# Column softmax of the first three batches from a ScalarE copy of the scores, in place of a second set of products

## The chip, the cores and the metric

The kernel runs on one core of a Trainium2 chip. The metric is the device time of one execution in microseconds (us). Times inside an execution come from the hardware profiler: they count from the start of the profiled span. The engines are named as the profile names them: PE (TensorE, matrix products; PEld its weight loads), DVE (VectorE), ACT (ScalarE), POOL (GpSimd) and SP (SyncE, which here only issues the stores).

## What is computed

Eight batches of an attention read in two directions, followed by a two-layer network with a squared ReLU:

```python
# x [8, 8, 512, 64], state [8, 8, 32, 64]: batch, head, token or state row, 64
scores  = scale * x @ state.T            # [.., 512, 32]
xread   = softmax(scores, rows)  @ state   # row softmax, over 32 state rows
scores2 = scale * state @ x.T            # [.., 32, 512]: the same scores, turned
sread   = softmax(scores2, rows) @ x       # column softmax, over 512 tokens
t = concat([xread, sread])               # 544 tokens a batch, heads side by side: [4352, 512]
out = (s * relu(t @ w_in)**2 + b) @ w_out  # 512 -> 2048 -> 512
```

The scores of both reads are the same numbers. The kernel makes them once per use, in a tile T of 128 partitions (4 heads x 32 state rows) by 2 groups x 512 tokens, fp32, in two banks of PSUM. T serves the row softmax (through a transpose) and, as it stands, the column softmax.

## The kernel before

The order of all instructions on every engine is written out by hand. The first stretch (lines 583 to 671) is a straight list for batches 0 and 1. Then the loop of lines 752 to 805 emits eight phases, b = 0 to 7. Phase b has sixteen steps (`phase`, line 674). A step runs the pieces that the lists `before` and `behind` hold for its number, then one slice of layer 1 for batch b + 1 (`layer1_x`: 2 matmuls into hps, a ReLU by ACT from hps to r), and every second step a square by DVE (`square`, r to g). Layer 2 of batch b (`layer2`, 4 matmuls of g with w_out into ops) is spread over the steps as pieces. In phases 6 and 7 layer 2 is computed with seven half-size products in place of eight (`fast_layer2`, products X, Y and W into opf tiles, sums of g by DVE). Phase 7 runs layer 1 of the sread rows. hps has two PSUM buffers, so the layer-1 slice i needs the ReLU of slice i - 2 done; r has five buffers.

The row softmax of batch b + 2 is a chain (`chain`, line 690), placed within phase b: `at_T` (16 small PE matmuls, T from stE and xT), `at_U` (DVE transposes T out of PSUM), `at_mu` (row maxima), `at_D` (Dm = U - mu), `at_E1` (ACT exponential), `at_z` (row sums and reciprocals), `at_At` and `at_A` (the weights A, scaled and transposed back by DVE). A is the moving operand of layer 1; its stationary operand M = state @ w_in (per head) is made by `at_M` (16 matmuls into mps) and copied to SBUF by `at_Mc`. xT is x transposed in 32 x 32 blocks by DVE (`at_xT`).

The column softmax of a batch is `at_nm` (DVE: maximum over 512 tokens, negated and scaled, nm and nms), `at_E2` (two ACT exponentials E of 512 columns that also give the sums rs), `at_a2` (DVE: times the reciprocal), `at_a2T` (8 PE transposes into aps and a copy), `at_V` (32 matmuls with x rows xn into vps) and `at_srd` (ACT copy into srdT). For batches 3 to 7 these pieces follow in the same phase as the chain, while T still stands in PSUM. For batches 0, 1 and 2 they run later, through `late` (line 707): batch 2 in phase 3 and batches 0 and 1 in phase 6. There T is long overwritten, so `late` begins with a second `at_T(b)` from a kept xT. The tiles xT_0, xT_1 and xT_2 have buffers of their own for that (lines 231 to 234); xT_3 and later share one.

T lives in either of two pairs of PSUM banks, made by `two_banks`: one (tag pt) for T and some M tiles, one (tag pa) for the second half of batch 0's T, most M tiles, aps and vps. PE's matmuls of a new tile there wait until the tile before it has been read.

In the first stretch batch 0 is done in two halves of its tokens (`at_T(0, 0)` in pt, `at_T(0, 1)` in pa). PE runs filler matmuls between (`idle`, tile dps). The weights w_in come in four DMAs from POOL's queue, and `at_M2(0, 2)` and `at_M2(0, 3)` need the last two.

Of the kernel before, what the change touches and what calls it, by code (L numbers as in the profile page):

```python
# [10 lines left out]
FP32 = mybir.dt.float32  # L11
FP16 = mybir.dt.float16
# [3 lines left out]
def kernel(  # L16
# [12 lines left out]
    nc = tc.nc  # L29
    AF = mybir.ActivationFunctionType  # L30
    ALU = mybir.AluOpType
    AX = mybir.AxisListType

    B, H, S, D = x.shape
# [3 lines left out]
    P = 128  # L38
    NK = DM // P
    NKF = DF // P  # L40
    NG = H // 4
# [10 lines left out]
    konst = ctx.enter_context(tc.tile_pool(name="konst", bufs=1))  # L52
    wpool = ctx.enter_context(tc.tile_pool(name="wpool", bufs=1))
    xpool = ctx.enter_context(tc.tile_pool(name="xpool", bufs=2))
    apool = ctx.enter_context(tc.tile_pool(name="apool", bufs=1))
# [30 lines left out]
    act, dve = nc.scalar.copy, nc.vector.tensor_copy  # L86
# [81 lines left out]
    def w_out_f(f):  # L168
        return w_out16[:, f, :]
# [34 lines left out]
    at = [dict() for _ in range(B)]  # L204
# [8 lines left out]
    def part(t, p=None, g=None):  # L213

        if g is not None:
            t = t[:, g : g + 1]
        if p is not None:
            n = t.shape[2] // 2
            t = t[:, :, n * p : n * p + n]
        return t  # L220
# [7 lines left out]
    def at_xT(b, g=None, p=None):  # L228

        if "xT" not in at[b]:  # L230
            keep = b < 3
            at[b]["xT"] = (konst if keep else apool).tile(
                [P, NG, S, 2], FP16, name=f"xT_{b}", tag=f"xTk{b}" if keep else "xT"
            )
        out = at[b]["xT"].rearrange("p g s e -> p g (s e)").bitcast(FP32)
        in_ = xh_t[b].rearrange("p g j d -> p g (j d)").bitcast(FP32)
        nc.vector.transpose(part(out, p, g), part(in_, p, g))  # L237

    def at_T(b, p=None):

        half = p is not None
        at[b]["T"] = T = two_banks(f"T_{b}", own=not p)
        for e in range(2):
            for hp in range(4):
                for g in range(NG):
                    r = hp ^ g
                    mm(
                        part(T[Ns * hp : Ns * hp + Ns], p, g)[:, 0, :],
                        stE[32 * r : 32 * r + 32, NG * b + g, :, e],
                        part(at[b]["xT"][32 * r : 32 * r + 32, :, :, e], p, g)[:, 0, :],  # L250
                        start=(e == 0), stop=(e == 1),
                        tp=(32 * r, Ns * hp),
                    )

    def at_U(b, p=None, g=None):
        U = sm(b, "U", [P, NG, S], FP32)
# [48 lines left out]

    def at_nm(b):
        nm, nms = sm(b, "nm", [P, NG], FP32), sm(b, "nms", [P, NG], FP32)
        nc.vector.tensor_reduce(  # L308
            nm, at[b]["T"], AX.X, ALU.max, negate=True
        )  # L310
        nc.vector.tensor_scalar(nms, nm, scale, None, ALU.mult)  # L311

    def at_E2(b, gs=range(NG)):
        E2, rs = sm(b, "E2", [P, NG, S], FP16), sm(b, "rs", [P, NG], FP32)
        for g in gs:
            nc.scalar.activation(  # L316
                E2[:, g], at[b]["T"][:, g], AF.Exp,
                bias=at[b]["nms"][:, g : g + 1], scale=scale, accum_out=rs[:, g : g + 1],
            )

# [88 lines left out]
    def layer1_half(b, f, p):  # L409

        M, A = at[b]["M"], at[b]["A"]
        hps = ps_h.tile([P, 2, HALF], FP32, name=f"hph_{b}_{f}_{p}", tag="ph")
        for i in range(2):
            for g in range(NG):
                lhsT = M[:, g, P * (f + i) : P * (f + i) + P]
                mm(hps[:, i, :], lhsT, part(A, p, g)[:, 0, :], start=(g == 0), stop=(g == NG - 1))
        r = R_t[b, f, p] = rpool.tile([P, 2, HALF], FP16, name=f"rh_{b}_{f}_{p}", tag="r")
        nc.scalar.activation(r, hps, AF.Relu)
# [10 lines left out]
    def layer2(tag, rr, q):  # L429
        if q == 0:  # L430
            ops_t[tag, rr] = ps_o.tile([P, DM], FP32, name=f"ops_{tag}_{rr}", tag="po")
        for f in range(4 * q, 4 * q + 4):
            nc.tensor.matmul(  # L433
                ops_t[tag, rr],
                G_t[tag][:, f, P * rr : P * rr + P],
                w_out_f(f),
                start=(f == 0),
                stop=(f == NKF - 1),
            )
# [150 lines left out]
    at_xT(0, 1, 0)  # L590
    at_xT(0, 0, 0)
    at_T(0, 0)
    T0 = at[0]["T"]
    at_xT(0, 1, 1)
    at_xT(0, 0, 1)
    at_T(0, 1)
    T1, at[0]["T"] = at[0]["T"], T0
    at_U(0, 0)
    at_mu(0, 0)
# [35 lines left out]
    at_U(1)  # L635
    layer1_half(0, 4, 1)
    layer1_half(0, 6, 1)
    layer2(0, 1, 0)
    square_half(0, 0, 1)
    square_half(0, 2, 1)  # L640
# [49 lines left out]
    def chain(b, s):  # L690
        return [
            (s[0], lambda: at_T(b)),
            (s[1], lambda: at_U(b)),
        ] + [
            (s[2], lambda: at_nm(b)),
            (s[3], lambda: at_E2(b, (0,))),
            (s[4], lambda: at_E2(b, (1,))),
        ] * (b > 2) + [
            (s[5], lambda: at_mu(b)),
            (s[6], lambda: at_D(b)),  # L700
            (s[7], lambda: at_E1(b)),
            (s[8], lambda: at_z(b)),
            (s[9], lambda: at_At(b)),
            (s[10], lambda: at_A(b)),
        ]

    def late(b, s):

        return [
            (s[0], lambda: at_T(b)),  # L710
            (s[1], lambda: at_nm(b)),
            (s[2], lambda: at_E2(b, (0,))),
            (s[3], lambda: at_E2(b, (1,))),
            (s[4], lambda: at_a2(b)),
            (s[5], lambda: at_a2T(b, dve)),
        ] + [(v, lambda: at_V(b)) for v in s[6:]] + [(v, lambda: at_srd(b)) for v in s[6:]]
# [35 lines left out]
    for b in range(0, B):  # L752
        if b in fast:
            before, behind = [], fast[b]
        else:
            before, behind = l2(b, 3 if b == 1 else 0) if b else ([], first())
        if b in (2, 4):
            for i, name in enumerate(("T1", "T2") if b == 2 else ("T3", "T4")):
                before += [(12 + 2 * i + h, lambda h=h, name=name: weight_sum(name, h)) for h in range(2)]
        behind = left + behind  # L760
        if b + 1 in FAST:
            sums, fast[b + 1] = fast_layer2(b + 1)
            before += [(14 + i, p) for i, p in enumerate(sums)]
        if b + 3 < B:
            before += [(2 if b else 5, lambda b=b: load_x(b + 3))]
        if b + 3 < B:
            before += [(13, lambda b=b: at_xT(b + 3))]
        if b and b + 2 < B:
            before += [(7, lambda b=b: load_xn(b + 2))]
        if b == B - 3:  # L770
            before += [(9, lambda: load_xn(0))]
        if b == B - 2:
            before += [(4, lambda: load_xn(1))]
        if b == 3:
            before += [(9, lambda: load_xn(2))]
        if b == 0:
            before += [(4, lambda: pair_states(4, NR)), (3, lambda: turn_states(4, 12, act)), (5, lambda: turn_states(12, NR, act))]
        if b + 2 < B:
            s = (1, 2, 3, 3, 4, 4, 5, 6, 7, 8, 9) if b else (5, 6, 7, 8, 9, 8, 9, 10, 11, 12, 13)
            before += [] if b else [(3, lambda: at_xT(2))]  # L780
            before += chain(b + 2, s)
            if b:
                before += [(7, lambda b=b: at_a2(b + 2))]
                before += [(10, lambda b=b: at_a2T(b + 2, act))]
        if b > 1 and b + 1 < B:
            bs = (b + 1, 2) if b == 4 else (b + 1,)
            v = 2 if b == B - 2 else 1
            before += [(v, lambda bs=bs: at_V(*bs))]
            before += [(v, lambda x=x: at_srd(x)) for x in bs]
        if b:  # L790
            plan = [(6 if b < B - 2 else 0, 1, [(b + 1, 3), (b + 2, 0)][: B - 1 - b])]
            plan += [(13 if b == 3 else 12, 1, [(b + 2, 1), (b + 2, 2)])] if b + 2 < B else []
            plan += [(1, 1, [(2, 2)])] if b == 1 else []
        else:
            plan = [(2, 0, [(1, 3)]), (10, 0, [(2, 0), (2, 1)])]
        for step, own, units in plan:
            make, copies, left = pieces(step, own, *units)
            before, behind = before + make, behind + copies
        if b == 3:
            before += late(2, (10, 11, 12, 12, 13, 15))  # L800
        if b == B - 2:
            before += late(0, (1, 2, 3, 4, 5, 6, 7)) + late(1, (6, 7, 8, 9, 10, 11, 12))
        phase(b + 1 if b + 1 < B else "sr", before, behind)
        if b and b not in fast:
            out_x(b, 3)
# [49 lines left out]
```

## Time and profile before

| what | value |
|---|---|
| median of 3 runs | 230.06 us (228.4, 230.11, 230.06) |
| the profiled execution | 229.42 us |
| its span, first to last instruction | 227.6 us |
| PE busy | 216.7 us (95%) |
| DVE busy | 175.1 us (77%) |
| ACT busy | 137.0 us (60%) |
| the second T of batches 2, 0 and 1 begins at | 114.80, 174.33 and 182.72 us |
| phases 0 to 7 begin about at | 33.3, 52, 75, 99, 124, 148, 173 and 194 us |

A row of the timeline reads: start, duration, engine, line, operation, output <- input, shapes, count of merged instructions, and in brackets the idle time of the engine just before with what ended it. The durations of matmuls overlap (a 128x512 matmul has 0.38 us in its row, and the next starts 0.215 us after it), so the cost of a group of matmuls on PE is read from start to start.

### The profile page before, as it was taken

What the parts mean: (1) busy time and instruction counts of PE and PEld (TensorE: products, weight loads), DVE (VectorE), ACT (ScalarE), POOL (GpSimd) and SP (SyncE); (2) the same over time, 40 slices, a digit from 0 to 9 for tenths busy, and PEclk for the clock granted to TensorE, in tenths of its full rate; (3) what the DMA queues carried; (4) which work ended last, traced back from release to release, by engine and by line L of the source; (5) the groups of instructions that cost most, each with busy time, mean ns of one, the idle gap of its engine ahead of it and who ended that gap; (6) DMA issues with size and microseconds to landing.
All of it is one profiled execution on the core that took longest, in us unless ns stands there. A gap on an engine that the chain in (4) does not pass through costs nothing.

```text
span 227.6 us, 4506 instructions
## 1 busy us (share of the span) xinstructions
PE 216.7 (95%) x1831; PEld 111.4 (49%) x1831; DVE 175.1 (77%) x268; ACT 137.0 (60%) x235; POOL 35.1 (15%) x65
## 2 busy tenths in 40 slices
PE   6597999999999999999999999999999999999982
PEld 2254334443444444444444535444544767788852
DVE  2688997887997598968896589969955996885430
ACT  2277676683797668757876478657866746423300
POOL 8431000106001500063002610030000400000000
PEclk9799999999999999999999999999999999999999
DMA  7999990724932862389527590437042610530272
GB/s 163 195 206 205 207 153 9 150 73 80 160 90 46 117 117 46 71 123 172 97 49 138 93 172 21 93 55 115 17 92 45 82 17 0 116 72 3 49 152 76
DMA packets 22920, 22.40 MB, mean 98 GB/s; under 512 B 4084, under 2 KB 16628, under 8 KB 22900
## 3 DMA queue, kind: packets, MB, share of 16 engines
q0 software_dynamic: 16640, 12.52, 38.1%
q1 hardware_dynamic: 5584, 9.44, 17.2%
q8 instruction: 14, 0.23, 0.4%
q10 hardware_dynamic: 676, 0.16, 0.3%
q14 instruction: 6, 0.05, 0.1%
HBM read 25.72 MB, written 8.91 MB: 152 GB/s over the span
## 4 chain that ended last, share of the span: by engine, by line
PE 86%; DMA 7%; DVE 3%; POOL 2%; issue 1%; ACT 0%; POOLq 0%
PE ops L433 35%; PE hps L395 24%; DMA w_in<-in_moe_w_in_dram 7%; PE opf_X L74 6%; PE mps L74 4%; PE hps_sr L395 3%; PE opf_W L74 3%; PE T L74 3%; PE vps L74 2%; PE ops_sr L817 2%; PE aps L74 2%; PE opf_Y L74 2%; PE ops_sr L433 2%; POOL xh L117 1%; POOL w_in L132 1%
## 5 line engine op out<-in xcount | busy, mean ns | idle before, releaser
L433 PE MATMUL ops<-w_out,g 128*128 128x512 f16 x384 | 97.9, 379 | 0.9 <-DMA w_out<-in_moe_w_out_dram 0.9
L398 ACT ACTIVATE r<-hps 128x512 f16<-128x512 f32 x120 | 71.0, 606 | 30.9 <-PE hps L395 30.3
L395 PE MATMUL hps<-A,M 128*128 128x512 f16 x240 | 70.2, 381 | 0.2 <-ACT r L398 0.2
L433 PEld LDWEIGHTS <-g 128*128 128x128 f16 x384 | 37.5, 98 | 46.0 <-issue 1.1
L403 DVE TENSOR_TENSOR g<-r 128x1024 f16<-128x1024 f16 x60 | 40.9, 682 | 15.9 <-ACT r L398 15.8
L395 PEld LDWEIGHTS <-M 128*128 128x128 f16 x240 | 20.8, 98 | 27.4 <-issue 8.7
L378 ACT CAST M<-mps 128x1024 f16<-128x1024 f32 x31 | 31.3, 1010 | 2.5 <-PE mps L74 2.3
L126 POOL DMA_DIRECT2D xn<-in_x_dram x32 | 18.5, 588 | 51.2 <-PE vps L74 50.3
L74 PEld LDWEIGHTS <-g 128*128 128x128 f16 x192 | 18.7, 98 | 4.8
L443 DVE SCALAR_TENSOR_TENSOR osb<-ops,sb_bc,bias_bc 128x512 f32<-128x512 f32 x24 | 17.9, 746 | 1.2 <-PE ops L433 1.2
L316 ACT ACTIVATE E<-T,nms 128x512 f16<-128x512 f32 x16 | 11.0, 687 | 5.7 <-DVE nms L311 5.7
L114 POOL COPY ahead<-xT 1x2 f16<-1x2 f16 x5 | 1.2, 250 | 84.0 <-DVE xT L237 68.1
L398 ACT ACTIVATE r_sr<-hps_sr 128x256 f16<-128x256 f32 x16 | 6.1, 383 | 13.0 <-PE hps_sr L395 12.9
L274 ACT ACTIVATE E<-Dm 128x1024 f16<-128x1024 f32 (+1 forms) x9 | 8.7, 963 | 8.6 <-DVE Dm L267 8.5
L257 DVE STREAM_TRANSPOSE U<-T 128x1024 f32<-128x1024 f32 (+1 forms) x9 | 10.1, 1124 | 3.4 <-PE T L74 3.4
L279 DVE TENSOR_REDUCE z<-E 128x32 f32<-128x1024 f16 (+1 forms) x9 | 9.9, 1099 | 2.8 <-ACT E L274 2.6
L237 DVE STREAM_TRANSPOSE xT<-xh 128x1024 f32<-128x1024 f32 (+2 forms) x12 | 10.2, 872 | 1.7 <-DMA xh<-in_x_dram 1.7
L74 PE MATMUL mps<-w_in,stT 64*32 64x512 f16 x256 | 11.2, 390 | 0.3 <-DMA w_in<-in_moe_w_in_dram 0.3
L360 ACT CAST srdT<-vps 128x128 f16<-128x128 f32 x8 | 5.7, 775 | 8.8 <-PE vps L74 8.8
L267 DVE TENSOR_TENSOR Dm<-U,mu 128x1024 f32<-128x1024 f32 (+1 forms) x9 | 9.9, 1100 | 0.1
L261 DVE TENSOR_REDUCE mu<-U 128x32 f32<-128x1024 f32 (+1 forms) x9 | 9.8, 1090 | 0.0
L308 DVE TENSOR_REDUCE nm<-T 128x2 f32<-128x1024 f32 x8 | 9.7, 1218 | 0.0
(76 smaller groups left out, 215.6 us busy)
## 6 DMA issues: line engine op xcount, KB each, us to landing
out_dram<-osb SPq DMA_DIRECT2D x40, 128.0 KB, 3.6
xn<-in_x_dram POOLq DMA_DIRECT2D x32, 128.0 KB, 6.3
xh<-in_x_dram POOLq DMA_DIRECT2D x15, 256.0 KB, 4.8
w_in<-in_moe_w_in_dram POOLq DMA_DIRECT2D x4, 512.0 KB, 12.8
w_out<-in_moe_w_out_dram POOLq DMA_DIRECT2D x4, 512.0 KB, 17.6
out_dram<-osx SPq DMA_DIRECT2D x16, 128.0 KB, 2.4
out_dram<-osb SPq DMA_DIRECT2D x4, 256.0 KB
xf<-in_x_dram SPq DMA_DIRECT2D x1, 512.0 KB, 3.5
```

The costliest lines, as they stand in the source:

```text
L74: return nc.tensor.matmul(out, lhsT, rhs, start=start, stop=stop, tile_position=tp, is_transpose=is_transpose, skip_group_check=skip,)
L126: nc.gpsimd.dma_start(out=xn_t[b][32 * jh : 32 * jh + 32].rearrange("t h c d -> t h (c d)"), in_=x[b].rearrange("h (t jh c) d -> jh t h (c ...
L237: nc.vector.transpose(part(out, p, g), part(in_, p, g))
L257: nc.vector.transpose(part(U, p, g), part(at[b]["T"], p, g))
L267: nc.vector.tensor_tensor(blk(part(Dm, p, g)), blk(part(at[b]["U"], p, g)), over_n(part(at[b]["mu"], p, g)), ALU.subtract,)
L316: nc.scalar.activation(E2[:, g], at[b]["T"][:, g], AF.Exp, bias=at[b]["nms"][:, g : g + 1], scale=scale, accum_out=rs[:, g : g + 1],)
L378: copy(at[b]["M"][:, :, 512 * j : 512 * j + 512], at[b]["mps", j])
L395: nc.tensor.matmul(hps, lhsT, rhs, start=(i == 0), stop=(i == len(terms) - 1))
L398: nc.scalar.activation(R_t[tag, f - f % 2][:, f % 2], hps, AF.Relu)
L403: nc.vector.tensor_mul(new_G(tag, r.shape[2])[:, f : f + 2], r, r)
L433: nc.tensor.matmul(ops_t[tag, rr], G_t[tag][:, f, P * rr : P * rr + P], w_out_f(f), start=(f == 0), stop=(f == NKF - 1),)
L443: nc.vector.scalar_tensor_tensor(osb, ops_t.pop((tag, rr)), s_bc, bias_bc, ALU.mult, ALU.add)
```

## The change

The second `at_T` is gone for batches 0, 1 and 2. In its place ACT copies T, 4 KB a partition, from PSUM to a kept fp32 tile Ts in SBUF while T is there for the row softmax (`at_keep`): for batch 0 in two halves, each right behind its `at_T`; for batch 1 behind the layer-1 halves 4 and 6 of the second half of batch 0; for batch 2 in phase 0, step 6. `at_nm` and `at_E2` of these batches read Ts. xT has one shared tile for all batches. Some pieces change their step: the exponential of batch 2's row softmax from 10 to 11 in phase 0, the M pieces (2, 0) and (2, 1) from 10 to 11, and of batch 1's late pieces nm from 7 to 6 and V from 12 to 13.

```diff
     def at_xT(b, g=None, p=None):
 
         if "xT" not in at[b]:
-            keep = b < 3
-            at[b]["xT"] = (konst if keep else apool).tile(
-                [P, NG, S, 2], FP16, name=f"xT_{b}", tag=f"xTk{b}" if keep else "xT"
-            )
+            at[b]["xT"] = apool.tile([P, NG, S, 2], FP16, name=f"xT_{b}", tag="xT")
...
+    def at_keep(b, p=None):
+
+        if "Ts" not in at[b]:
+            at[b]["Ts"] = konst.tile([P, NG, S], FP32, name=f"Ts_{b}")
+        act(part(at[b]["Ts"], p), part(at[b]["T"], p))
+
...
     def at_nm(b):
         nm, nms = sm(b, "nm", [P, NG], FP32), sm(b, "nms", [P, NG], FP32)
-        nc.vector.tensor_reduce(
-            nm, at[b]["T"], AX.X, ALU.max, negate=True
-        )
+        T = at[b].get("Ts", at[b]["T"])
+        nc.vector.tensor_reduce(nm, T, AX.X, ALU.max, negate=True)
...
-                E2[:, g], at[b]["T"][:, g], AF.Exp,
+                E2[:, g], at[b].get("Ts", at[b]["T"])[:, g], AF.Exp,
...
     at_T(0, 0)
     T0 = at[0]["T"]
+    at_keep(0, 0)
     at_xT(0, 1, 1)
     at_xT(0, 0, 1)
     at_T(0, 1)
+    at_keep(0, 1)
     T1, at[0]["T"] = at[0]["T"], T0
     at_U(0, 0)
...
     at_U(1)
     layer1_half(0, 4, 1)
     layer1_half(0, 6, 1)
+    at_keep(1)
     layer2(0, 1, 0)
...
     def late(b, s):
 
         return [
-            (s[0], lambda: at_T(b)),
             (s[1], lambda: at_nm(b)),
...
-            s = (1, 2, 3, 3, 4, 4, 5, 6, 7, 8, 9) if b else (5, 6, 7, 8, 9, 8, 9, 10, 11, 12, 13)
+            s = (1, 2, 3, 3, 4, 4, 5, 6, 7, 8, 9) if b else (5, 6, 7, 8, 9, 8, 9, 11, 11, 12, 13)
             before += [] if b else [(3, lambda: at_xT(2))]
             before += chain(b + 2, s)
+            before += [] if b else [(6, lambda: at_keep(2))]
...
-            plan = [(2, 0, [(1, 3)]), (10, 0, [(2, 0), (2, 1)])]
+            plan = [(2, 0, [(1, 3)]), (11, 0, [(2, 0), (2, 1)])]
...
-            before += late(0, (1, 2, 3, 4, 5, 6, 7)) + late(1, (6, 7, 8, 9, 10, 11, 12))
+            before += late(0, (1, 2, 3, 4, 5, 6, 7)) + late(1, (6, 6, 8, 9, 10, 11, 13))
```

As built, the transposes U of batch 0's two halves wait for the ACT copies of the same halves; the copies of batches 1 and 2 wait for the transposes U of theirs. On every engine all else keeps its order but for the moved steps above.

## The prediction, on record before the run

> **What bounds the kernel now.** I read the page first: shares, clock and the chain that ended last.
>
> ```profile
> span 227.6 us, 4506 instructions
> PE 216.7 (95%) x1831; PEld 111.4 (49%) x1831; DVE 175.1 (77%) x268; ACT 137.0 (60%) x235; POOL 35.1 (15%) x65
> PEclk9799999999999999999999999999999999999999
> PE 86%; DMA 7%; DVE 3%; POOL 2%; issue 1%; ACT 0%; POOLq 0%
> ```
>
> PE is the bound: 86% of the chain is PE work. The table by stretches has PE busy in every instant from 33.3 to 215.9 us. The chain of waits in order of time says where it is not PE: until 20.7 us it runs through the issue and landing of the third w_in transfer, and from 21.8 to 28.3 us through batch 1's transposes. The waits of PE come next.
>
> ```profile
> PE mps L74 <- DMA w_in<-in_moe_w_in_dram: 0.3, 1, 0.3
> PE hps L395 <- ACT r L398: 0.2, 1, 0.2
> ```
>
> After the start there is one short wait, for a ReLU of ACT. So whatever leaves PE's list between 33 and 216 us shortens the run by its pitch, as long as ACT and DVE can follow the faster PE; and whatever is put on ACT costs only where a ReLU or a square comes too late.
>
> **The products removed.** Three second at_T of 16 matmuls: at 114.80 (batch 2, phase 3), 174.33 (batch 0) and 182.72 us (batch 1, phase 6). The timeline of phase 6 gives the price, best read by comparing a step with T and one without:
>
> ```profile
> 181.31 1.04 PE L74 MATMUL opf_X<-w_T,g 128*128 128x256 f16 x8
> 182.18 0.61 PE L74 MATMUL aps<-ident,a 128*128 128x128 f16 x8
> 182.72 0.64 PE L74 MATMUL T<-xT,stE 32*32 32x512 f16 x16
> 183.30 0.61 PE L395 MATMUL hps<-A,M 128*128 128x512 f16 x2
> ...
> 189.70 0.61 PE L74 MATMUL aps<-ident,a 128*128 128x128 f16 x8
> 190.15 0.60 PE L395 MATMUL hps<-A,M 128*128 128x512 f16 x2
> ```
>
> From the start of aps to the start of hps it is 183.30 - 182.18 = 1.12 us with T and 190.15 - 189.70 = 0.45 without: T costs 0.67, its 0.58 and 0.09 for the change to the small products. Likewise in phase 3, 115.37 - 114.26 = 1.11, so 0.66; and at 173.37, where X to hps takes 1.54 and without T 0.87 (177.40 to 178.27), 0.67. Sum: **-2.0 us** of PE. Its lower bound is the three T by the chain's own pitch, 3 x 0.57 = 1.71.
>
> Can the others follow? DVE is the tight one in phase 6:
>
> ```profile
> 177.00:182.00 5.00, 5.00 (x40) 3.71 (x40) 4.93 (x11) 4.01 (x9) 2.30 (x4) 1.00 0.74 86
> 182.00:187.00 5.00, 5.00 (x82) 3.42 (x80) 4.97 (x10) 2.05 (x5) 0.00 (x0) 1.00 0.16 23
> ```
>
> The columns are stretch, length, then PE, PEld, DVE (4.93 and 4.97 of 5 us), ACT and POOL. But its run of work from 176.43 begins behind an idle 1.18 us that ended with product X, so it starts earlier with PE: everything up to a2 of batch 0 (ends 182.30) moves by 0.67 as a block with aps. After the second T is gone PE is 1.34 ahead. The eviction of X at step 6 then is the first late one, since nm of batch 1 now stands ahead of it: a2T at 182.16 to 182.85, nm and nms to 184.2, a square to 184.9, the eviction to 185.6. The third X needs that bank at 187.53 - 1.34 = 186.2, so 0.6 is left. a2 of batch 1 waits for ACT, which follows PE, and V is a step later, so its copy a2T gets a step more. I take no loss here, and 0.5 at most for each T as its other end. In phase 3 DVE has nm of batch 2 at 116.04 to 117.26 behind its own queue; the exponentials and the ReLU of step 12 end 0.3 us earlier than before in place of 0.66, and that ReLU's bank is needed 1.1 us later. No loss.
>
> **The copies added on ACT.** No row copies 1024 fp32 from PSUM to fp32 in SBUF. Nearest are M (1024 fp32 from PSUM to f16, 1010 ns, the next instruction 0.89 after its start) and the exponential E (fp32 from SBUF, 1057 ns); the far end is DVE's transpose U with its fp32 output, 1247 ns. I take M's. [...]
>
> *Batch 0.* U of each half now waits for the copy of that half. The first T ends at 8.66; the copy (ACT is idle, half size: 0.63 by the half-size E) ends at 9.34; U starts at 9.39 in place of 8.76.
>
> ```profile
> 8.76 0.68 DVE L257 STREAM_TRANSPOSE U<-T 128x512 f32<-128x512 f32 x1
> 19.35 1.05 PE L74 MATMUL hph<-A,M 128*128 128x256 f16 x8 [0.16 <-DVE A L304]
> 20.75 0.41 PE L74 MATMUL mps<-w_in,stT 64*32 64x512 f16 x8 [0.35 <-DMA w_in<-in_moe_w_in_dram]
> ```
>
> DVE runs without a gap, so A of half 0 ends at 14.03 + 0.63 = 14.66, against hph at 14.58, which has filler matmuls ahead of it: 0.14 late. The ReLUs, E1, A of half 1 and the hph of 19.35 follow 0.15 late, and then PE waits 0.35 for w_in at 20.75 anyway. Cost 0; without that cover 0.15 (up to 0.63 if the fillers gave none). The second copy (to 10.07) lies ahead of U's turn at 11.44.
>
> *Batch 1.* The copy follows the ReLU that ends at 23.39, and U is done at 23.06; behind it wait ReLUs 8 and 9, 0.45 late (24.04 to 24.5). ACT is idle for 1.5 us before 26.67 and PE needs ReLU 8 at 26.44. Cost 0.
>
> *Batch 2*, phase 0, where ACT is busy:
>
> ```profile
> 41.33 1.25 DVE L257 STREAM_TRANSPOSE U<-T 128x1024 f32<-128x1024 f32 x1 [0.57 <-PE T L74]
> 43.56 0.60 ACT L398 ACTIVATE r<-hps 128x512 f16<-128x512 f32 x1 [0.64 <-PE hps L395]
> 44.20 0.68 DVE L403 TENSOR_TENSOR g<-r 128x1024 f16<-128x1024 f16 x1
> 44.22 1.03 PE L395 MATMUL hps<-A,M 128*128 128x512 f16 x4
> 48.15 1.00 ACT L378 CAST M<-mps 128x1024 f16<-128x1024 f32 x1
> 54.22 0.69 DVE L403 TENSOR_TENSOR g<-r 128x1024 f16<-128x1024 f16 x1
> 55.04 1.03 PE L433 MATMUL ops<-w_out,g 128*128 128x512 f16 x4
> ```
>
> The copy waits for U (42.58), so it runs from 42.63, and ReLU 6 behind it from 43.52 to 44.12, ReLU 7 to 44.62 (was 44.16). hps 8 and 9 at 44.22 and 44.66 need exactly these: 0 to 0.05 late, 0.25 with the 1.25 us copy. DVE feels it: the square of 44.20 starts at 44.66, and Dm, E1, z, At, A and the squares behind them move by 0.46. A ends at 53.54, needed at 54.4: free. The last square ends at 55.37 in place of 54.91. PE on its side gains: the exponential and the M pieces a step later put ReLU 13 ahead, and the 0.2 wait goes. So layer 2 would reach the third matmul of the 55.04 group (g of slice 14) at 55.28 in place of 55.47, and waits 0.14 for the square. Sum of phase 0: -0.19 + 0.14, about **0**, up to +0.4.
>
> *Sharing xT* costs nothing: xT of batch 1 is written at 19.22, the T that read batch 0's ended at 9.4; batch 3's at 51.24, T of batch 2 ended at 41.3. Ts in SBUF changes nm (1218 ns against 1211 of the maximum over U) and E by some 25 ns (E1 631, ReLU 606), off the path.
>
> **Sum.** -2.0 (T) + 0 (batches 0 and 1) + 0 (phase 0) + 0.1 for small slips = -1.9. The profiled execution took 229.42 us (span 227.6 and 1.8 around it), so 227.5; span 225.7. The median of the runs shown is 230.06, against which -1.9 gives 228.2; their spread (228.4 to 230.11) is nearly as large as the change.
>
> **Rivals.**
>
> *ACT and DVE give part back.* For: DVE's 4.97 of 5 us, a2 of batch 0 ends within PE's aps, ACT's queue in phase 0. Against: those queues start behind PE. Price: two T of phase 6 by half, +0.67, and phase 0 at +0.4: -2.0 + 1.1 = -0.9, 228.5.
>
> *The copy of batch 2 turns it slower.* Place: ReLUs 6 and 7 behind it, then the DVE chain to the square at 54.22. Each us beyond my 1.0 reaches PE in full at hps 8 and 9. It decides when the copy takes 1.0 + 1.9 = 2.9 us; at 4 us the time is 229.42 - 1.9 + 3.0 = 230.5, and 1% slower needs 5.2. Against: no ACT row of that size is over 1.06.
>
> *U behind the copy is not covered.* For: if w_in lands 0.4 us earlier than at 20.75, the start is bound by that chain. Price 0.15 to 0.63: 227.7 to 228.2. [...]
>
> *The gain is larger*: a PE ahead of DVE's stores, or an earlier w_in, gives another 0.7: 226.8. Nothing in the waits of PE speaks for it.
>
> **Chances.** Forecast (226.9 to 228.2) 0.6; part given back 0.16; U uncovered 0.08; larger 0.08; slower than before 0.08, of which 0.05 by over 1%. 1% (2.3 us) is about what a measurement of this kernel can tell from no change. The forecast of 1.9 us is 0.8%, close below that, so with the spread of the runs a third of its weight and all of the larger gain count as faster: 0.3; within 1% 0.65; slower 0.05. Range 226.3 to 229.5: from the larger gain, less spread, to the part given back against the higher median.
>
> **What would show it.** Right: PE has 48 fewer T matmuls; phase 6 shorter by 1.3 us and phase 3 by 0.66; aps to hps 0.45 in both; mps of 20.75 in its place, still behind w_in; hps 8 and 9 of phase 0 without a wait over 0.1; about 0.15 for the square in the third or fourth matmul of the first layer-2 group of phase 1. Wrong: a wait of hps for r above 0.3 in phase 0; aps waiting for a2, or opf for an eviction, in phase 6; U of batch 0 ending the wait ahead of mps; a copy over 1.3 us.

## The result, and the profile after

| | before | after |
|---|---|---|
| median of 20 runs each | 229.28 us | 228.12 us |
| lowest to highest | 228.4 to 231.83 | 226.19 to 229.08 |
| the profiled execution | 229.42 us | 228.19 us |
| its span | 227.6 us | 226.4 us |

The ratio of the times is 0.9941, with an interval of 0.992 to 0.9962: 0.6% faster, some 1.35 us; the medians alone are 1.16 us apart. The forecast was 1.9 us less, 227.5. A second series of the changed kernel, further down, gave 0.994 (0.9912 to 0.9969).

The page of the changed kernel, its lines on the span, the engines, the clock and the chain:

```profile
span 226.4 us, 4413 instructions
PE 216.0 (95%) x1783; PEld 111.1 (49%) x1783; DVE 175.8 (78%) x268; ACT 139.8 (62%) x239; POOL 35.2 (16%) x65
PEclk9769999999999999999999999999999999999999
PE 88%; DVE 5%; DMA 3%; ACT 1%; issue 1%; POOLq 0%
```

PE has the 48 matmuls less, but only 0.7 us less busy time, where the three T alone were 2.0 us. The clock line says where to look: its third digit (11.3 to 17 us) was 9 and is 6. In the chain DMA has gone from 7% to 3%: w_in no longer ends the start. The waits of PE (line, releaser, then total us, times, longest us):

```profile
PE hph L74 <- DVE A L307: 1.1, 1, 1.1
...
PE sbps L74 <- DVE U L260: 0.2, 1, 0.2
```

The wait of mps for w_in is gone from the list. In its place stand a wait of 1.1 us for A and one of 0.2 us for U. The list has one wait for a ReLU of layer 1, and it is that of before (0.24 at 28.26, now at 29.16), not a new one of phase 0.

**Behind the start everything is as forecast.** One number separates the two parts: the span from the start of batch 1's T to the end. Before it is 227.60 - 21.09 = 206.51 us, after 226.41 - 21.99 = 204.42: 2.09 less, against the 1.9 to 2.0 of the sum. From the T of one phase to that of the next, 0.05 of it is phase 0, 0.68 phase 3 and 1.37 phase 6 with its neighbours. The timeline of phase 6:

```profile
180.80 1.04 PE L74 MATMUL opf_X<-w_T,g 128*128 128x256 f16 x8
181.68 0.61 PE L74 MATMUL aps<-ident,a 128*128 128x128 f16 x8
182.12 0.59 PE L397 MATMUL hps<-A,M 128*128 128x512 f16 x2
...
188.52 0.61 PE L74 MATMUL aps<-ident,a 128*128 128x128 f16 x8
188.96 0.59 PE L397 MATMUL hps<-A,M 128*128 128x512 f16 x2
```

From aps to hps it is 0.44 us at both places, where it was 1.12 and 0.45. DVE is as full as before (busy time of PE, PEld, DVE, ACT and POOL in two stretches of 5 us, then the clock), and PE does not stop:

```profile
177.00:182.00 5.00, 5.00 (x45) 3.93 (x43) 4.93 (x11) 3.69 (x9) 2.12 (x4) 1.00 0.84 107
182.00:187.00 5.00, 5.00 (x69) 3.58 (x66) 4.96 (x9) 3.33 (x7) 0.00 (x0) 1.00 0.01 1
```

Phase 0, with the copy of batch 2:

```profile
43.51 1.01 ACT L256 COPY Ts<-T 128x1024 f32<-128x1024 f32 x1 [0.19 <-DVE U L260]
44.42 1.09 ACT L400 ACTIVATE r<-hps 128x512 f16<-128x512 f32 x2
45.12 1.04 PE L397 MATMUL hps<-A,M 128*128 128x512 f16 x4
...
55.57 0.69 DVE L405 TENSOR_TENSOR g<-r 128x1024 f16<-128x1024 f16 x1
55.72 1.20 PE L435 MATMUL ops<-w_out,g 128*128 128x512 f16 x4
```

The copy takes 1.01 us, and hps 8 and 9 (45.12) start without a wait. The four ops matmuls at 55.72 take 1.20 where the same group before took 1.03: the third waits about 0.15 for the square of 55.57. What pays for it is four steps earlier: the four hps matmuls at 50.99 took 1.19 before, with a stop for ReLU 13 among them, and at 51.84 take 1.03.

**The start lost 0.90 us between these two profiles.** Batch 1's T begins at 21.99 in place of 21.09. The timeline of the start after:

```profile
8.34 1.25 ACT L256 COPY Ts<-T 128x512 f32<-128x512 f32 x2 [0.77 <-PE T L74]
8.96 0.72 DVE L260 STREAM_TRANSPOSE U<-T 128x512 f32<-128x512 f32 x1 [0.51 <-ACT Ts L256]
11.04 0.71 DVE L260 STREAM_TRANSPOSE U<-T 128x512 f32<-128x512 f32 x1
11.80 0.58 PE L74 MATMUL sbps<-sb_one,ones 1*128 1x2 f32 x2 [0.20 <-DVE U L260]
12.31 1.89 PE L582 MATMUL dps<-ones 128*128 128x512 f16 x4
15.90 1.04 PE L74 MATMUL hph<-A,M 128*128 128x256 f16 x8
20.68 1.05 PE L74 MATMUL hph<-A,M 128*128 128x256 f16 x8 [1.09 <-DVE A L307]
21.65 0.41 PE L74 MATMUL mps<-w_in,stT 64*32 64x512 f16 x8
```

and the same places before:

```profile
10.81 0.71 DVE L257 STREAM_TRANSPOSE U<-T 128x512 f32<-128x512 f32 x1
12.14 0.54 PE L74 MATMUL sbps<-sb_one,ones 1*128 1x2 f32 x2
12.61 1.04 PE L580 MATMUL dps<-ones 128*128 128x512 f16 x4
14.58 1.04 PE L74 MATMUL hph<-A,M 128*128 128x256 f16 x8
```

U waits for the copy, as foreseen. What was not foreseen is the row of sbps: these two matmuls of two columns, which broadcast the scalars (`spread_scalars`), go into the pair of banks that the second U reads (tag pa), and wait 0.20 for it. Before, that U ended at 11.52 and sbps came at 12.14, 0.62 later. The four fillers behind sbps then take 1.89 us, where the same four took 1.04 before (12.61). They run at half clock. The table by stretches of the changed kernel, from 12 us on, with the granted clock in the third column from the right:

```profile
13.00:14.00 1.00, 1.00 (x3) 0.15 (x1) 0.97 (x2) 0.00 (x0) 0.41 (x1) 0.50 1.13 203
...
15.00:16.00 1.00, 1.00 (x4) 0.40 (x3) 0.56 (x1) 0.84 (x1) 0.54 (x1) 0.58 1.25 208
```

and of the kernel before:

```profile
12.00:13.00 1.00, 1.00 (x12) 0.67 (x5) 0.93 (x3) 0.72 (x1) 0.00 (x0) 0.75 1.09 203
13.00:14.00 1.00, 1.00 (x12) 0.30 (x11) 0.97 (x3) 0.36 (x2) 0.74 (x1) 1.00 1.15 204
```

By the clock's record PE has half clock from 9.09 to 12.51 before (3.41 us) and from 9.02 to 15.85 after (6.83 us, twice as long). hph of half 0 so starts at 15.90 in place of 14.58, its ReLUs are late, the second half's exponential stands behind them in ACT's list, and A of half 1 ends 1.1 us after PE needs it. The chain in order of time, a part:

```profile
12.38 1.82 PE dps L582 x4
...
16.07 0.45 PE hph L74 x4
...
16.54 1.08 ACT rh L420 x2
17.62 0.53 ACT E L277
...
19.91 0.72 DVE A L307
```

This chain, with sbps ahead of it and hph of 20.68 behind, ends the start at 21.99, after w_in, which has become one of the covered things. The third transfer of w_in, issued at 5.23 in both, landed after 14.8 us, so near 20.0; before it took 15.5, to 20.7.

### The profile page after: what moved, and what is told of

Same layout as the page of the kernel before. It is cut to its first block, busy times and chain, and to the rows that moved or that the text cites. A ratio compares the mean times of both kernels' runs of the same rounds, so it can differ in the third digit from the quotient of the medians.

```text
span 226.4 us, 4413 instructions
## 1 busy us (share of the span) xinstructions
PE 216.0 (95%) x1783; PEld 111.1 (49%) x1783; DVE 175.8 (78%) x268; ACT 139.8 (62%) x239; POOL 35.2 (16%) x65
## 4 chain that ended last, share of the span: by engine, by line
PE 88%; DVE 5%; DMA 3%; ACT 1%; issue 1%; POOLq 0%
PE ops L435 35%; PE hps L397 23%; PE opf_X L74 6%; PE mps L74 4%; PE hps_sr L397 3%; PE opf_W L74 3%; DMA xh<-in_x_dram 3%; PE vps L74 2%; PE T L74 2%; PE ops_sr L822 2%; PE aps L74 2%; PE opf_Y L74 2%; PE ops_sr L435 2%; PE dps L582 1%; DVE U L260 1%; DVE Dm L270 1%
## 5 line engine op out<-in xcount | busy, mean ns | idle before, releaser
L582 PE MATMUL dps<-ones 128*128 128x512 f16 x20 | 9.0, 617 | 1.4 <-DVE ones L150 1.4
L318 ACT ACTIVATE E<-T,nms 128x512 f16<-128x512 f32 x10 | 6.9, 688 | 4.3 <-DVE nms L313 4.3
```

The costliest lines, as they stand in the source:

```text
L582: nc.tensor.matmul(dps, ones16[:, :P], ones16, start=True, stop=True)
```

## The experiments

Three theories for the 0.90 us, as the expectations name them. **A**: U behind the copy makes PE stop at sbps; the gap keeps PE at half clock for one more stretch of 3.41 us, and the slow fillers make the start late. **B**: the 0.63 us by which U, and with it the DVE chain to A, is late is itself the price. **C**: it is no effect of the change but the chance of one execution, in which the half-clock stretch was long or w_in late. "Rest" below is the time from the start of batch 1's T to the end of the span: 206.51 before, 204.42 after. "Before" in each ratio are runs of the kernel before, on the same chip.

**1. U first.** The copies of batch 0 go behind its first U.

```diff
     T0 = at[0]["T"]
-    at_keep(0, 0)
...
     at_T(0, 1)
-    at_keep(0, 1)
     T1, at[0]["T"] = at[0]["T"], T0
     at_U(0, 0)
+    at_keep(0, 0)
+    at[0]["T"] = T1
+    at_keep(0, 1)
+    at[0]["T"] = T0
     at_mu(0, 0)
```

> The changed kernel, but of batch 0's first half the transpose U reads T before the ScalarE copy does; no work is taken out. The profiles of before and of the changed kernel differ in two places: 2.08 us gained where the three T stood, and 0.9 us lost in the start (T of batch 1 at 21.99 us in place of 21.09, with a stretch of 6.8 us at a granted clock of 0.5 in place of 3.4). Theory A (clock): U behind the copy is late, the tiny product sbps waits 0.20 for it, PE has a gap, and the stretch at half clock is granted for longer, which slows the fillers ahead of the first layer-1 product. Theory B (chain): the start is late by the delay of U itself, carried through the DVE chain. Theory C (chance): the length of the half-clock stretch changes from execution to execution in both kernels and the copies cost the start nothing. A and B: about -2.0 us against before, 0.6 better than the changed kernel. C: as the changed kernel, -1.3.

Measured: 0.9898 (0.9866 to 0.9931), 227.2 against 229.23 us. Its timeline:

```profile
8.79 0.72 DVE L260 STREAM_TRANSPOSE U<-T 128x512 f32<-128x512 f32 x1
9.55 1.07 ACT L256 COPY Ts<-T 128x512 f32<-128x512 f32 x2 [2.30 <-DVE U L260]
12.11 0.58 PE L74 MATMUL sbps<-sb_one,ones 1*128 1x2 f32 x2
12.63 1.50 PE L582 MATMUL dps<-ones 128*128 128x512 f16 x4
...
15.06 1.04 PE L74 MATMUL hph<-A,M 128*128 128x256 f16 x8
```

sbps does not wait, and PE has full clock at 13.60, where the record of the clock begins; the four fillers before that take 1.50, between the 1.04 at full and the 1.89 at half clock. hph starts at 15.06, batch 1's T at 21.15. The rest is 204.42, to the hundredth that of the changed kernel. So the start hangs on the order of two reads of one bank; A and B both allow that.

**2. The copies alone.** The kernel before, with two copies at the start that nobody reads.

```diff
+    def at_keep(b, p=None):
+
+        if "Ts" not in at[b]:
+            at[b]["Ts"] = konst.tile([P, NG, HALF], FP32, name=f"Ts_{b}")
+        act(at[b]["Ts"], part(at[b]["T"], p))
...
     T0 = at[0]["T"]
+    at_keep(0, 0)
...
     at_T(0, 1)
+    at_keep(0, 1)
```

> The kernel before with the two copies of batch 0 added at the same places and read by nobody (both into one half-size tile); the second T products all stay. A and B: 0.6 to 0.9 us slower than before. C: within 0.2 of before.

Measured: 1.003 (1.0002 to 1.0059), 230.03 against 229.23 us, so 0.8 by the medians, as A and B expected. The twelve executions fall into two groups: six at 228.44 to 229.45 us, and six at 230.62 to 231.17, above every one of the 23 of the kernel before (at most 230.6). The profile is of the first group; its clock is full at 10.68, where the record begins, before PE comes to sbps:

```profile
18.77 1.05 PE L74 MATMUL hph<-A,M 128*128 128x256 f16 x8 [0.73 <-DVE A L310]
20.81 0.41 PE L74 MATMUL mps<-w_in,stT 64*32 64x512 f16 x8 [1.00 <-DMA w_in<-in_moe_w_in_dram]
```

Here U is late, the clock is not, and PE still waits 1.00 us for w_in; batch 1's T starts at 21.15, the rest is 206.49. So the lateness alone is covered in this execution, as the prediction had it. That is against B, by which it costs every execution. What the six slow ones lost is not profiled: two of them have a mean clock of 0.985, the long stretch of A (see 8), and in the others, at 0.998 to 1.0, the record does not show one.

**3. A filler in the gap.** One of the four fillers behind sbps goes ahead of it.

```diff
     at_M2(0, 0, True)
+    idle(1)
     spread_scalars()
-    idle(4)
+    idle(3)
```

> The changed kernel with one of the four filler matmuls behind sbps moved ahead of it, so that PE has work while sbps waits for U; U stays behind the copy, the number of fillers is the same. A: the gap goes, the half-clock stretch is short again, -1.9 against before. B: no change from the changed kernel, -1.3, for U is as late. C: -1.3.

Measured: 0.9883 (0.9855 to 0.9911), 226.75 against 229.23 us; the half-clock stretch lies at 7.74 to 11.15, batch 1's T starts at 20.66, the rest is 204.42. U is as late as in the changed kernel. By the time this is for A. Its place beside the kernel before is not the filler's doing (control, 5). But the profile can't tell what the filler did, for PE was at full clock before it came to sbps (12.06), and one profile says little on how often the clock stays low; see 12.

**4. Batch 0 as before.** The changed kernel, with a second T for batch 0 and no copies at the start.

```diff
     T0 = at[0]["T"]
-    at_keep(0, 0)
...
     at_T(0, 1)
-    at_keep(0, 1)
...
-        return [
+        return [(s[0], lambda: at_T(b))] * (b == 0) + [
             (s[1], lambda: at_nm(b)),
```

> The changed kernel with batch 0 as in the kernel before: no copies in the start, its xT kept, its second T made in phase 6; batches 1 and 2 use their copies. A and B: the start is as before and two T are gone: 2 x 0.67 + 0.05 = -1.4. C: two thirds of the changed kernel's gain, -0.9. The start's profile should show T of batch 1 near 21.1 by A and B.

Measured: 0.9973 (0.9952 to 0.9994), 228.58 against 229.23 us: -0.6 where I expected -1.4. The clock is as before (half from 9.08 to 12.49), batch 1's T starts at 21.69 behind a wait of 1.29 for w_in. But the rest is 205.67, where two removed T should leave 206.51 - 0.68 - 0.67 = 205.16. A loss of 0.5 us behind the start that neither theory knows; 7 and 9 follow it up.

**5. The filler, control.** The edit of 3 in the kernel before.

> Control for the moved filler: the kernel before with one of the four fillers moved ahead of sbps, nothing else. sbps has no wait there in the profile of before. If the moved filler only closes the gap that the copies open (theory A), nothing changes: within 0.3 us of before. If the filler's new place is worth time by itself, it is 0.4 us faster, and then so much of the gain of the changed kernel with the moved filler is not the cure of the start.

Measured: 1.0013 (0.9994 to 1.0031), 229.4 against 229.14 us, rest 206.52. Without the copies the filler is worth nothing. Its profile shows something else: batch 1's T starts at 21.99, as late as in the changed kernel, here behind a wait of 1.19 for w_in that landed late. So 21.99 in one profile is by itself no sign of the change; C is right that far.

**6. Both edits**, 1 and 3, in the changed kernel.

> The changed kernel with both edits: U of batch 0's first half ahead of its copy, and the filler ahead of sbps. By A each edit alone removes the gap ahead of sbps, so both together give no more than the better one: -2.0 to -2.5 us against before. By B (delay of the DVE chain) the first edit adds up to 0.6 to the second: -3.0.

Measured: 0.9911 (0.9892 to 0.993), 227.29 against 229.14 us, batch 1's T at 20.66 behind a wait of 1.42 for w_in, rest 204.43. No better than either alone. In this profile sbps still waits for U, and longer than in the changed kernel, but at full clock, which the record has from 5.50 on:

```profile
10.56 0.38 PE L74 MATMUL sbps<-sb_one,ones 1*128 1x2 f32 x2 [0.41 <-DVE U L260]
```

No half clock follows, and w_in ends the start.

**7. No copies at the start.** The changed kernel; the column softmax of batch 0 reads batch 1's copy, so that the sread rows of batch 0 come from other scores.

```diff
-    at_keep(0, 0)
...
-    at_keep(0, 1)
...
-        T = at[b].get("Ts", at[b]["T"])
+        T = at[max(b, 1)].get("Ts", at[b]["T"])
```

> The changed kernel without the two copies of batch 0; batch 0's column softmax reads batch 1's copy instead, so its sread rows are computed from the wrong scores and all later work keeps its size. The start is that of before and all three T are gone: -2.1 us by A and B. If the missing part of the changed kernel's gain lies elsewhere (theory C, or a loss behind the start), -1.3.

Measured: 0.9963 (0.9941 to 0.9985), 228.06 against 229.14 us: -0.85 where I expected -2.1. The start is right (half clock 7.87 to 11.29, T at 21.13), but the rest is 205.00, 0.58 more than the changed kernel's. Half of that is in phase 0, where ReLU 10 starts late, and a square that layer 2 waits 0.29 for with it:

```profile
46.01 0.59 PE L397 MATMUL hps<-A,M 128*128 128x512 f16 x2
47.02 0.60 ACT L400 ACTIVATE r<-hps 128x512 f16<-128x512 f32 x1 [0.97 <-PE hps L397]
```

In the changed kernel the same ReLU starts 0.69 after its product, at 47.55, here 1.01 after it. Most of the other half is one wait of PE for a ReLU, 0.23 us at 132.56, in phase 4. ACT's work there is the same in both kernels; two instructions fewer stand ahead of it in ACT's list.

**8. The changed kernel again**, for how often the clock stays low.

> The changed kernel once more, for a second profile of its start: -1.3 us against before. By A the start's T of batch 1 goes with the length of the half-clock stretch: near 21.1 to 21.3 us with one stretch of 3.4 us, near 22 with 6.8. By B it is late by the same 0.4 to 0.9 with either.

Measured: 0.994 (0.9912 to 0.9969), 227.88 against 229.14 us, as in the first series. Its profile has batch 1's T at 22.44 and rest 204.44. The record of its clock begins only at 17.05, at full clock; the four fillers take 1.89 as in the first profile, so PE is at half clock there. No wait is listed at sbps, but from the M matmuls to sbps it is 0.70 us (10.91 to 11.61) where it was 0.56 before: PE stops for 0.14, until U is done.

```profile
11.61 0.58 PE L74 MATMUL sbps<-sb_one,ones 1*128 1x2 f32 x2
12.12 1.89 PE L582 MATMUL dps<-ones 128*128 128x512 f16 x4
```

A long stretch shows in the mean clock of a whole execution. Where the record covers it, that clock is 0.985 in the profile of the changed kernel, 0.983 in run 10 and 0.981 in run 12, against 0.992 with a stretch of 3.41 us (before, runs 3, 4, 7, 9 and 11); 3.41 us at half of 227 are 0.0075. So 0.986 or less is counted as a long stretch here. Of the 30 executions of this kernel 12 are that low, of 73 of the kernel before 5, of 40 of runs 4, 5, 7 and 9, which have no late U, 3. Against C. In these 30 the median with a low clock is 228.28 us and that of the others 227.50. The count is a lower bound: the profile of this run has a long stretch, but its record of the clock begins late, and its mean reads 0.996.

**9. Two tiny copies.** The kernel of 7, with two ACT copies of two columns at the places of the removed ones.

```diff
+    tiny = konst.tile([P, 2], FP16, name="tiny")
...
     T0 = at[0]["T"]
+    act(tiny, ident16[:, 0:2])
...
     at_T(0, 1)
+    act(tiny, ident16[:, 2:4])
```

> The kernel without start copies (batch 0's column softmax reads batch 1's copy, its sread rows are computed from the wrong scores) with two tiny ScalarE copies of 2 columns at their places. That kernel lost 0.57 us behind the start (span less the start of batch 1's T: 205.00 us, against 204.42 in every kernel with the start copies), where ReLU 10 of phase 0 started 0.32 later after its product. If the place of an instruction in ScalarE's list sets that loss, the tiny copies restore it: 204.42, and -2.1 us against before. If the missing data or tile sets it: 205.00 again and -0.9.

Measured: 0.9909 (0.9885 to 0.9933), 227.45 against 229.3 us, half clock 8.38 to 11.79, T at 21.30, rest 204.39. Two copies that cost nothing restore the 0.6 us that 7 lost, so that loss came with the place of the later instructions in ACT's list, not with the copies' data. That the 0.5 of run 4 is the same loss is likely (phase 0 is 0.29 longer in both) but was not tried. With U not late, this is the changed kernel without the price of its copies at the start: against C.

**10. The gap alone.** The kernel before, no copy in it; two of the fillers ahead of M and sbps go behind them, so that sbps comes before U is done.

```diff
     at_E1(0, 0)
-    idle(5)
+    idle(3)
     at_M2(0, 0, True)
     spread_scalars()
-    idle(4)
+    idle(6)
```

> The kernel before with two of its five fillers moved from ahead of the first M products to behind sbps: PE then comes to sbps about 0.3 us before U is read, and has a gap there, without any copy. Theory A: the half-clock stretch is longer in a good part of the executions, 0.2 to 0.8 us slower than before, and slower executions at a granted clock of 0.985. If the copies act otherwise than by the gap: within 0.2 of before.

Measured: 1.0027 (1.0008 to 1.0046), 230.13 against 229.3 us; 6 of 12 executions at a clock of 0.986 or less. Its timeline:

```profile
10.76 0.58 PE L74 MATMUL sbps<-sb_one,ones 1*128 1x2 f32 x2 [0.63 <-DVE U L257]
11.28 2.74 PE L580 MATMUL dps<-ones 128*128 128x512 f16 x6
...
20.77 1.05 PE L74 MATMUL hph<-A,M 128*128 128x256 f16 x8 [1.10 <-DVE A L304]
```

Half clock from 9.39 to 16.21, batch 1's T at 22.08, the wait for A 1.10 as in the changed kernel, rest 206.52. A gap at sbps with DVE on time gives the whole picture. This is the strongest run for A. Its gap is three times that of the changed kernel (0.63 against 0.20), and the edit opens a second one of 0.23 ahead of M at 9.50, where PE now waits for w_in.

**11. The copy of batch 2 twice**, in the kernel of 3.

```diff
-            before += [] if b else [(6, lambda: at_keep(2))]
+            before += [] if b else [(6, lambda: at_keep(2)), (6, lambda: at_keep(2))]
```

> The changed kernel with the moved filler (best so far: -2.5 us, span less start of batch 1's T 204.42 us) with the copy of batch 2 made twice in a row in phase 0. The prediction's claim is that what the copy takes beyond about 1.0 us reaches PE in full at the products of slices 8 and 9: ReLU 6 and 7 are 0.9 later, so 0.85 more behind the start, 205.3, and -1.6 us against before. If ScalarE's queue has more slack than that: 204.4 to 204.7.

Measured: 0.9967 (0.9946 to 0.9987), 228.39 against 229.3 us, rest 205.46, 1.04 more. In its timeline:

```profile
42.79 2.06 ACT L256 COPY Ts<-T 128x1024 f32<-128x1024 f32 x2 [0.19 <-DVE U L260]
...
45.40 1.08 PE L397 MATMUL hps<-A,M 128*128 128x512 f16 x4 [0.84 <-ACT r L400]
```

From batch 2's T to hps 8 it is 4.61 us, where the changed kernel has 3.61: all but 0.04 of the loss is there (0.84 of it is idle time by the row). The step in phase 0 is right: one copy of 1.0 us fits, and a second reaches PE in full.

**12. The filler again**, the kernel of 3.

> The changed kernel with one filler ahead of sbps, once more: -2.1 to -2.5 us against before, and 0.8 to 1.1 us faster than the changed kernel as it is; span less start of batch 1's T 204.42 us.

Measured: 0.9918 (0.9889 to 0.9946), 227.19 against 229.3 us, T at 21.95, rest 204.41. This time its profile has a long stretch, 9.41 to 16.24:

```profile
11.09 0.61 PE L582 MATMUL dps<-ones 128*128 128x512 f16 x1
11.77 0.58 PE L74 MATMUL sbps<-sb_one,ones 1*128 1x2 f32 x2
```

U ends at 11.72, and sbps starts right behind it, 0.68 us after the filler, where run 11 with the same start has 0.54: one filler is not always enough. Of 14 executions of 3 and 12 two have a clock of 0.986 or less, and with the 12 of run 11 it is 6 of 26. So 3 alone had been a lucky series, and by the count the filler is not shown to cure the start.

**The versions beside each other.** Ahead of both kernels are 1 (0.9898), 3 and 12 (0.9883 and 0.9918) and 6 (0.9911). Each is 0.8 to 1.2% faster than before; among each other, and 1, 6 and 12 beside the changed kernel, their intervals overlap. In 1 and 6 none of 12 executions had the low clock. 1 is the plain one: no filler to tune, and U does not wait.

## Why the prediction was right, and where it was not

*The products removed*, -2.0: right. 0.68 in phase 3 and 1.37 in phase 6, 0.44 us from aps to hps at both places.

*DVE and ACT can follow*: right. DVE is busy for 4.93 and 4.96 of 5 us, and no aps, hps or opf of phase 6 waits for it. The rival "part given back" did not come.

*The copy of batch 2*: right in size (1.01 against M's 1.01) and in its place. The square reached PE 0.15 late as worked out, the gain of ReLU 13 paid for it, and phase 0 came out 0.05 shorter. (The 0.2 in the prediction's list of waits is not this stop: that wait lies at 28.26, still in the start, and is there after too. The stop for ReLU 13 is the 0.16 inside the group of 50.99.) "Each us beyond my 1.0 reaches PE in full" was measured as 1.04 for a second copy (1.05 more of ACT's time).

*The copy of batch 1*: cost 0, right. From batch 1's T to batch 2's it is 41.51 - 21.99 = 19.52 us, as before (40.61 - 21.09).

***Batch 0, "Cost 0"*: this is the step that failed.** That U is 0.63 late was right (it starts 1.11 after T in place of 0.52, so 0.59), and so was the cover as such: run 2 has it in its profile, with w_in still the last at 20.81. But the sum followed the late U only down DVE's list to A and hph. The second U is also awaited by PE, at sbps, which no row of the trace before shows waiting: its slack there was 0.62 us, no more than the 0.63 by which U was to be late, and I never looked at it. In the profile after PE reached that point some 0.6 us earlier than before (its M at 10.97 in place of 11.58; 0.4 of that because the first T was earlier, 7.85 in place of 8.24), and the wait came out at 0.20. The rival "U uncovered" had the right place and a price of 0.15 to 0.63, and named as its condition that w_in lands 0.4 earlier. In the profiled execution it did land 0.7 earlier (20.0), but what came is a delay through the clock, larger than that price: 0.90 us against the kernel before, and more against that w_in. Over the executions it is less, since it comes in part of them: 228.28 us at a low clock and 227.50 otherwise, 0.78 apart, in at least 12 of 30. Without it the kernel is 227.50 - 229.23 = 1.7 us ahead of the kernel before at its usual clock, close to the forecast of 1.9. That the other figure of the forecast, 228.2 against the median of 230.06, lies so near the 228.12 measured is luck: that median of three runs was 0.8 above the median of twenty, and this made up for the loss at the start.

What is shown and what is not: that a gap at sbps, without any copy, makes the long stretch more frequent (6 of 12 against 5 of 73) and the run slower is shown by run 10. That the changed kernel's loss is this one rests on the profiles. All fourteen sort the same way. Where PE is at half clock and nothing stops it, it takes 0.54 to 0.56 us from the instruction ahead of sbps to sbps (before, runs 1, 4, 5, 9 and 11). It takes 0.83 in the changed kernel, 0.70 in run 8, 0.68 in run 12 and 1.26 in run 10, and in these four half clock goes on for one more step. In runs 2, 3, 6 and 7 PE is at full clock when it comes to sbps; it stops there for 0.12, 0.04 and 0.41 in 2, 3 and 6, and no half clock follows. Two pairs compare the two outcomes with the steps at the same place: the half clock of the kernel before and of run 4 ends at 12.51 and 12.49, that of the changed kernel at 15.85, 3.34 later; that of run 1 ends at 13.60 and that of run 8, the changed kernel again, at 17.05, 3.45 later. Both are within 0.1 us of one step of 3.41.

The 0.90 of the two profiles is no measure of the loss. Where w_in ends the start, batch 1's T begins anywhere from 20.66 (run 6) to 21.99 (run 5), and the changed kernel's 21.99 lies within that. By its own w_in, which landed near 20.0, its T could have begun near 20.4 (an estimate: before, T follows the landing at 20.71 by 0.38), so that execution lost up to 1.6. The 0.78 between executions at a low clock and the others is the better figure. With how much idle time the second step comes can't be told from these runs. Idle time alone does not decide it: run 3 is at half clock from 7.74, waits for T until 7.90, and has full clock one step later.

*U's order.* The 0.63 was worked out for the order as built, the copy first. In both orders the second reader of a bank starts where the first ends: in the changed kernel U at 8.96 behind the copy of 8.34, with U first (run 1) the copy at 9.55 behind the U of 8.79 to 9.51. So with U first it is the copy that waits, and nobody needs the copy until phase 6.

## What to carry to other kernels

A late result must be followed to all its readers, and to every writer that needs its bank, not only down the chain that looks longest: here two matmuls of two columns were the ones hit, by 0.20 us. Where one engine's read of a bank waits for another's, as U did here (0.59 late behind the copy), the reader on the path goes first and the copy for later second. And while PE was still at half clock at this start, a gap of a tenth or two came with a loss of many times its length (0.14 us in run 8 and 0.20 in the changed kernel, against 0.78): the span from a fixed instruction to the end tells such a loss from the effect of the change itself.

## What the runs showed of the hardware

Where the record of the clock covers the start, half clock came in whole steps: 3.41 us before and in runs 3, 4, 7, 9 and 11, 6.83 in the changed kernel, run 10 and run 12, always at 0.50, at a place that differs by execution (the single steps end at 11.15, 11.29, 11.79, 12.40, 12.49 and 12.51). Ahead of the second step PE works but for short stops: in the changed kernel and in runs 8 and 12 it is busy for 0.80, 0.93 and 0.93 of the us from 11 to 12 and all of those from 9 to 11 and 12 to 13, and stops at sbps for 0.1 to 0.3 us (0.83, 0.70 and 0.68 us from the instruction ahead of sbps to sbps, against 0.54 to 0.56). Executions at a low clock are 0.78 us of 227 slower than the others, 0.3%, and that is more than half of the 1.35 us that this change brings.

Two instructions fewer at the head of ACT's list, at 8 to 10 us, made a ReLU at 47 us start 0.32 us late, with the same work around it (7), and two tiny copies in their place cured it (9); 0.6 us in all. What in the list's layout does that is open; no row of the trace shows it.
